# Written instruction lists for four queues of a fused GateLoop and multiplicative-FFN kernel

## The chip, the cores and the metric

The kernel runs on one NeuronCore of a Trainium2 chip. The metric is the device time of one execution in microseconds. A core has five engines that fetch instructions from queues of their own, each strictly in the order in which the queue stands: TensorE (PE, whose weight loads are shown as PEld), VectorE (DVE), ScalarE (ACT), GpSimd (POOL) and SyncE (SP), which here only issues transfers. An instruction that waits for a semaphore holds up everything behind it on its own queue. Transfers that SP and POOL issue are carried out by the same 16 DMA engines.

## The reference, cut to what matters

Two blocks follow each other. The first is a gated linear recurrence with complex gates, for 4 batches, 8 heads, 768 steps and a head width of 48; the second is a feed-forward block whose two products are multiplied element by element.

```
mag = sqrt(a_re**2 + a_im**2)
scale = minimum(mag, 0.999) / (mag + 1e-06)
a_re_n, a_im_n = a_re * scale, a_im * scale
for t in range(S):                      # S_re, S_im: 48 x 48 per head
    new_re = ar * S_re - ai * S_im
    new_im = ar * S_im + ai * S_re
    S_re, S_im = new_re + k[t] v[t]^T, new_im
    y[t] = q[t] @ S_re
x = y, heads beside each other          # 3072 x 384
h = (x @ w1) * (x @ w2) @ w3            # d_ff = 1024
out = h @ w_out
```

The products of w3 and w_out are joined once, since nothing stands between them, so a token costs three matrix products.

## The kernel before, in words

A **unit** is one half of one batch's sequence: 384 steps, all 8 heads. There are 8 units, numbered from 0. Three kinds of work belong to a unit.

**Gates** (`gates` for units 0 and 1, `gates_apart`, lines 598 to 768, from unit 2 on). From the gates `re` and `im` of a unit the kernel makes, on ACT and DVE in turn, the running magnitude and the running angle: logarithm and exponentials on ACT, scans on DVE, then cosine and sine on ACT. The steps that are named later are, in their order: `im_` (L645, im times the reciprocal of re) and `sq_` (L647), `n_` (L653), `min_` and the magnitude scans (L664, L667), `z4_` and `r2_` (L675, L677), the angle scans (L686), `k_` (L702, k times the reciprocal magnitude), `z5_` (L708, the angle cut to one turn, from which ACT at L636 makes abs, cos and sin), `q_` (L716), and four products: `kc_` (L750, k times cosine, tile gR), `qc_` (L753, q times cosine, tile gA), `ks_` (L758, k times sine, in k) and `qs_` (L764, q times sine, in q). Each is done in two parts, one of 384 and one of 768 elements per partition.

**Attention** of a unit on PE: transposes of gR and k (`tp`, L991, copied to KT by ACT at L993), the state products (`kv`, L1069, added to T by DVE at L1075), the scores (`sc`, L1004, whose masked copy to A is DVE's COPY_PREDICATED at L1007), and the outputs (`y`, L1043, copied by ACT and DVE to x0 and x1 at L1047 and L1050; POOL makes x2 at L1051).

**Feed-forward** of a unit on PE: the products `m` (L1089), with evictions by ACT (L1123, L1130) and DVE (`ab`, L1105), and the products `o` (L1184), copied by ACT (L1188) and written out. PE does the feed-forward of unit u-1 while the other engines prepare the gates of unit u.

Once per unit, gR, k, gA and q are moved into a layout by head: twelve transfers on SP (L740) into KL and QL, which the scores read. The unit's v is loaded into `vr` by POOL's queue (L569) and spread by seven more SP transfers into `V` (L591), which `y` reads. The next unit's `re` and `im` come over SP (L527); the next unit's k and q over POOL's queue, released when the last `y` of the unit before has been read.

From unit 3 on the feed-forward uses weights that are split in two parts. The split (`split_ops`, L1152 on ACT, L1155 and L1157 on DVE) runs once, while unit 2 is prepared.

What sets the order: PE's queue is written out by hand as one sequence of pieces. For the other queues the program steps through that sequence and keeps a clock for each engine; `fill`, `fits` and the cost tables (TIMES, WIDE, SCAN, PASS) decide behind which PE piece the next gate step is put, and a table (PLAN) does so for the first 36 pieces. Inside `tc.manual_schedule` the order in which the program text is run is the order of the queue. Before that block, in the stage that joins w3 and w_out and makes unit 0's gates, a scheduler orders the four queues.

Of the kernel before, what the change touches and what calls it, by code (L numbers as in the profile page):

```python
# [21 lines left out]
ORDER = mybir.DependencyInfo(mybir.DependencyClass.NoSync, mybir.DependencyReason.DATA)  # L22
# [352 lines left out]
        f()  # L375


@with_exitstack
def kernel(
    ctx: ExitStack,  # L380
# [32 lines left out]

    nc = tc.nc
    B, H, D, S = qt.shape
    P = 128
    C = 128
# [32 lines left out]
    weights_pool = ctx.enter_context(tc.tile_pool(name="weights", bufs=1))  # L452
    w3o = weights_pool.tile([P, KF, DM], FP, name="w3o")
    ident = weights_pool.tile([P, P], FP, name="ident")
    make_identity(nc, ident)
    good = weights_pool.tile([1, 1], I32, name="good")

    fast = ExitStack()
# [81 lines left out]
    def take(u, x):  # L540
        t = slot(u, x, x)
        g_t.setdefault(u, {})[x] = t[:, :, 0:TT] if x == "q" else t
# [54 lines left out]
    chained, paced = [], []  # L597

    def chain(ins):

        if chained and not paced:
            tc.add_manual_dep(ins.ins, chained[-1].ins.name, ORDER, reason="tables")
        chained[:] = [ins]

    def gate_head(u):
# [762 lines left out]
    def rounding():  # L1368

        stack = ExitStack()  # L1370
        for n, k in (("raw", 2), ("low", 2), ("w3s", 2), ("early", 1)):
            cv[n] = stack.enter_context(tc.tile_pool(name=n, bufs=k))
        return stack
# [25 lines left out]
    def w12_early():  # L1399
        if w1.dtype != FP:  # L1400
            w12_load(0, slice(0, 2), ("q", "k"))
# [23 lines left out]
    def row_load(f, parts=1):  # L1425

        step = FF // parts
        w3_t[f] = fetch([columns(w3t, 0, step)[:, f:f + 1], words(wo)[:, f:f + 1]] +
                        [columns(w3t, n * step, (n + 1) * step)[:, f:f + 1] for n in range(1, parts)],
                        {0: "KL", 1: "QL"}.get(f % 4))  # L1430
# [306 lines left out]
    with tc.manual_schedule(engines={mybir.EngineType.PE}):  # L1737

        phase = rounding()
        row_load(0, 4)  # L1740
        load_gates(0)
        row_load(1, 2)
        row_load(2)
        row_load(3)
        take(0, "q")
        take(0, "k")
        steps = gates(0, True)
        for f in range(KF):
            row_work(f)
            if f == 0:  # L1750
                load_of(0, "k")
                load_of(0, "q")
            if f + 4 < KF:
                row_load(f + 4)
            if f == VLOAD:
                load_v(0)
                w12_early()
            if f == KF - 1:
                continue
            for j in range(KF):  # L1760
                fuse(f, j)
            step(steps, (3, 2, 2, 2, 1, 1, 0)[f])
        for _ in steps:
            pass
        for j in range(KF // 2):
            fuse(KF - 1, j)
        fills = [("f7", lambda j=j: [fuse(KF - 1, j + x) for x in range(2)]) for j in range(KF // 2, KF, 2)]
        gate["ops"] = gates(1, False)
        chain(nc.scalar.preload_act_table_set("natural_log_exp_and_others"))
        with tc.manual_schedule(engines={mybir.EngineType.Activation, mybir.EngineType.DVE, mybir.EngineType.Pool, mybir.EngineType.SP}):  # L1770

            paced.append(True)
            clock.update(PE=0.0, ACT=0.0, DVE=0.0, POOL=0.0, SP=3.0, DMA=8.0)
            landings[:] = [0.0] * RING
            ready.clear()
            ready.update({"moves": 9.0, ("raw", 0): 0.0, ("re", 1): 2.0})
            w12_load(0, slice(len(got) and got[0][0][0].stop, KD))
            turn_v(0)
            w12_load(1)
            rest = ffn(0)  # L1780
            urgent.append([None, w12_ops()])

            def head(i):
                if i % 4 == 0:
                    force(i // 4)
                rest[i][1]()
                if i == HEAD - 1:
                    phase.close()
                    late.append(fast.enter_context(tc.tile_pool(name="late", bufs=1)))
                    late.append(fast.enter_context(tc.tile_pool(name="looks", bufs=1)))  # L1790
                    looks.append(check_weights(late[1]))
                    ops = split_ops()
                    splitting.append([next(ops), ops])
            seq = mixed([x for p in pieces(0) for x in p], fills, FILLS[0]) + [("begin", 0)] + [(rest[i][0], lambda i=i: head(i)) for i in range(HEAD)]
            for u in range(1, NU):
                seq += unit(u, rest[HEAD:] if u == 1 else ffn(u - 1), AHEAD[u])
            seq += ffn(NU - 1)
            advance()
            run(seq[:-4] + [("judge", 0)] + seq[-4:-2] + [("judge", 1)] + seq[-2:])
    fast.close()  # L1800

    value = nc.values_load(good[0:1, 0:1], min_val=0, max_val=1)
    with tc.If(value == 0):
        general(tc, qt, kt, v, art, ait, w1, w2, w3t, wo, w3o, ident, out)

# [35 lines left out]
```

## Time and profile before

| | before |
|---|---|
| median of 3 runs | 534.02 us |
| range of the runs | 533.82 to 536.47 us |
| profiled execution: first to last instruction | 534.5 us |
| PE busy | 498.3 us, 93% |
| DVE busy | 374.7 us, 70% |
| ACT busy | 325.6 us, 61% |
| POOL busy | 254.0 us, 48% |
| mean granted TensorE clock | 0.993 |

The profiled execution's own time is known as its span; the median of the unprofiled runs is 0.5 us below it. A row of a timeline reads: start, length, engine, line, operation, output<-inputs, sizes, count, and in brackets the idle time of that engine just before the row with what ended it. Busy times of PE are modelled at a matmul's end, so a short wait can be hidden in them.

### The profile page before, as it was taken

The page shows a single profiled execution, that of the slowest core. Times are in us where ns is not written, and L with a number is a line of the kernel's source. Part 1 is how long each engine was busy: PE and PEld are TensorE (multiplying, and loading weights), DVE is VectorE, ACT ScalarE, POOL GpSimd, SP SyncE. Part 2 cuts the span into 40 slices and gives each one's busy share as a digit, 9 for nine tenths or more (in the row PEclk, how much of TensorE's full clock was granted, in tenths as well). Part 3 has the DMA queues.
Part 4 walks back from the last instruction along what each step waited for, and adds up shares of the span by engine and source line. Part 5 has one row for each costly group of instructions (what it writes and reads, how often), then busy time and mean ns, then how long its engine had stood idle before and what let it go on. Part 6 is the DMA issues. An engine that isn't in the chain of part 4 may idle for free.

```text
span 534.5 us, 13643 instructions
## 1 busy us (share of the span) xinstructions
PE 498.3 (93%) x5594; PEld 378.1 (71%) x5594; DVE 374.7 (70%) x607; ACT 325.6 (61%) x569; POOL 254.0 (48%) x317
## 2 busy tenths in 40 slices
PE   5689889999998999988999999999999998999995
PEld 2355565556655679957888688967896787878972
DVE  7999699855779988756773876577657837336750
ACT  6979866665675458982587557855786554213420
POOL 1000000028968886752664765487457458415510
PEclk9899999999999999998999999999999999999999
DMA  8999859692379219791599239932993176716611
GB/s 258 369 400 286 189 161 307 126 232 72 79 174 229 73 56 234 157 219 40 126 236 216 77 82 245 225 90 70 229 232 87 40 209 169 205 43 189 200 50 37
DMA packets 66424, 89.75 MB, mean 168 GB/s; under 512 B 29872, under 2 KB 53872, under 8 KB 65584
## 3 DMA queue, kind: packets, MB, share of 16 engines
q1 hardware_dynamic: 57904, 59.15, 44.0%
q0 software_dynamic: 8448, 29.63, 20.3%
q8 instruction: 46, 0.75, 0.6%
q14 instruction: 26, 0.21, 0.1%
HBM read 61.01 MB, written 4.72 MB: 123 GB/s over the span
## 4 chain that ended last, share of the span: by engine, by line
PE 51%; DVE 17%; DMA 13%; issue 6%; ACT 5%; POOL 5%; SPq 1%; POOLq 0%; DVEq 0%; ACTq 0%
PE m L1089 24%; PE o L1184 16%; PE y L1043 4%; PE sc L1004 4%; DMA k<-in_k_dram 3%; DMA KL<-k 3%; PE kv L1069 2%; DVE gR L750 2%; PE tp L991 2%; DMA QL<-q 2%; DMA q<-in_q_dram 2%; DMA look<-in_a_re_dram 1%; DVE gA L753 1%; DMA raw<-in_w_dram 1%; POOL look L1327 1%
## 5 line engine op out<-in xcount | busy, mean ns | idle before, releaser
L1184 PE MATMUL o<-w3o,ab 128*128 128x384 f32 x384 | 131.7, 492 | 0.0
L1089 PE MATMUL m<-x,low 128*128 128x384 f32 x576 | 119.2, 339 | 0.0
L1089 PEld LDWEIGHTS m<-x,low 128*128 128x128 f32 x576 | 102.6, 188 | 0.2 <-ACT m L1123 0.2
L1184 PEld LDWEIGHTS o<-w3o,ab 128*128 128x128 f32 x384 | 70.4, 190 | 45.6 <-issue 2.4
L1105 DVE TENSOR_TENSOR ab<-m,ab 128x384 f32<-128x384 f32 x64 | 35.1, 553 | 57.2 <-PE m L1089 39.4
L1089 PE MATMUL m<-x,wh 128*128 128x384 f32 x288 | 69.6, 350 | 3.4 <-ACT ab L1130 2.4
L1123 ACT ACTIVATE m<-m 128x384 f32<-128x384 f32 x96 | 45.5, 476 | 36.0 <-PE m L1089 35.6
L1089 PE MATMUL m<-xT,ws 128*128 128x384 f32 x192 | 63.1, 487 | 1.2 <-ACT xT L1054 1.2
L1328 POOL TENSOR_SCALAR look<-look 128x192 f32<-128x192 f32 (+1 forms) x55 | 54.4, 988 | 5.0
L1089 PEld LDWEIGHTS m<-x,wh 128*128 128x128 f32 x288 | 50.8, 188 | 7.4 <-ACT ab L1130 3.6
L1325 POOL TENSOR_TENSOR look<-look 128x256 f32<-128x256 f32 (+1 forms) x43 | 31.9, 743 | 50.1 <-DMA look<-in_w_dram 32.3
L1089 PEld LDWEIGHTS m<-xT,ws 128*128 128x128 f32 x192 | 36.0, 190 | 25.6 <-ACT xT L1054 1.7
L1273 POOL MEMSET seen<- 128x256 bf16 x1 | 0.3, 317 | 107.7 <-DVE ab L1105 107.7
L1007 DVE COPY_PREDICATED A<-mask,sc 128x512 f32<-128x512 uint8 x48 | 32.8, 734 | 26.5 <-PE sc L1004 26.5
L1289 POOL TENSOR_TENSOR seen<-seen,look 128x192 bf16<-128x192 bf16 (+1 forms) x55 | 44.3, 805 | 4.5
L1051 POOL TENSOR_TENSOR x<-x,x 128x384 fp32r<-128x384 f32 x18 | 23.1, 1284 | 41.7 <-DVE x L1050 41.5
L1188 ACT COPY ot<-o 128x384 f32<-128x384 f32 x24 | 11.4, 476 | 48.4 <-PE o L1184 48.2
L1043 PE MATMUL y<-A,V 128*32 128x128 f32 x768 | 40.2, 276 | 0.6 <-issue 0.6
L1004 PEld LDWEIGHTS sc<-QL,KL 96*32 96x32 f32 x1536 | 29.2, 112 | 13.6 <-issue 8.7
L1004 PE MATMUL sc<-QL,KL 96*32 96x32 f32 (+3 forms) x1536 | 32.8, 238 | 4.4 <-DMA QL<-q 3.0
L1043 PEld LDWEIGHTS y<-A,V 128*32 128x32 f32 x768 | 35.0, 112 | 1.5 <-issue 1.5
L1043 PE MATMUL y<-QL,T 96*32 96x128 f32 x640 | 35.6, 275 | 0.0
(163 smaller groups left out, 909.2 us busy)
## 6 DMA issues: line engine op xcount, KB each, us to landing
looked<-in_w_dram POOLq DMA_DIRECT2D x14, 512.0 KB, 4.5
look<-in_w_dram POOLq DMA_DIRECT2D x27, 256.0 KB, 5.0
raw<-in_w_dram SPq DMA_DIRECT2D x6, 1024.0 KB, 10.3
KL<-gR SPq DMA_DIRECT2D x24, 192.5 KB, 3.6
KL<-k SPq DMA_DIRECT2D x24, 192.5 KB, 7.1
QL<-gA SPq DMA_DIRECT2D x24, 192.0 KB, 8.2
QL<-q SPq DMA_DIRECT2D x24, 192.0 KB, 7.9
raw<-in_w_dram SPq DMA_DIRECT2D x6, 768.0 KB, 6.1
```

The costliest lines, as they stand in the source:

```text
L1004: nc.tensor.matmul(out=sc[SB * g:SB * g + SB, j, s0:C], lhsT=KL[:, x * n + j, w][:, s0:s0 + SB], rhs=QL[:, x * n + j, w][:, s0:C], start=T ...
L1007: last["sc", u, c, x] = nc.vector.copy_predicated(out=A[:, x * n:(x + 1) * n], data=sc, mask=mask)
L1043: nc.tensor.matmul(out=o, lhsT=a, rhs=b, start=s0, stop=s1)
L1051: nc.gpsimd.tensor_tensor(out=x[2], in0=x[1], in1=x[0], op=OP.subtract)
L1089: nc.tensor.matmul(out=out, lhsT=a, rhs=b, start=start and i == 0, stop=i == len(terms) - 1, skip_group_check=not start)
L1105: last["ab", u, j] = nc.vector.tensor_tensor(out=ab_t[u][:, j], in0=m, in1=ab_t[u][:, j], op=OP.mult)
L1123: nc.scalar.activation(out=got[m], in_=got[m], func=AF.Copy, scale=1.0 + 1.0 / BITS)
L1184: nc.tensor.matmul(out=m, lhsT=ab_t[u][:, f, t * P:(t + 1) * P], rhs=w3o[:, f], start=(f == 0), stop=(f == KF - 1))
L1188: nc.scalar.copy(out=o, in_=m)
L1289: nc.gpsimd.tensor_tensor(out=seen[:, 0:n], in0=seen[:, 0:n], in1=x, op=OP.add)
L1325: tt(out=x, in0=x, in1=x, op=OP.mult)
L1328: ts(out=x, in0=x, scalar1=low, scalar2=None, op0=OP.is_ge)
```

## The change

Each call on ScalarE, VectorE, GpSimd and SyncE now goes through a small recording layer (`Logged`, `Log`), which keeps the instructions of each queue in the order in which the program text made them. The block that put these four queues in that order is gone, and so is the rule that chained ACT's table-dependent instructions. In its place stand written lists, one for each queue: a number n > 0 takes the n-th instruction of those that are left, a number -n takes the next n as they stand. `in_order` ties each instruction to the one before it in the list, with a dependency that costs no semaphore. All recorded instructions have the line of the recording layer, L385. The computation, the tiles, the transfers and their sizes are the same.

```diff
+class Log:
+    def __init__(self, engine):
+        self.engine, self.log = engine, []
+    def __getattr__(self, name):
+        def call(*args, **kw):
+            self.log.append(getattr(self.engine, name)(*args, **kw))
+            return self.log[-1]
+        return call
...
+ORDERS = dict(
+    scalar="""
+9 -15 3 3 3 -2 1 1 1 1 -4 2 -5 8 8 -2 3 -2 1 -9 4 -1 3 -4 6 6 6 -2 4 -1 3 3 3 3 -4 4 -99 5 -2 1 2 -5 1 -4 1 -4 1 -1
...
+""", gpsimd="""
+
+""", sync="""
+-99 8 8 7 9 9 8 -2 4 6 6 7 7 5 5 1 1 -9 4 4 1 1 -4 2 2 1 2 2 1 2 2 1 -5 7 7 7 8 8 8 9 9 -1 9 9 7 7 -1 4 1 1 -7 8 8 7
...
+def in_order(tc, log, order):
+    left, before, taken = list(log), None, []
+    for n in map(int, order.split()):
+        taken += [left.pop(n)] if n > 0 else [left.pop(0) for _ in range(-n)]
+    for ins in taken + left:
+        if before:
+            tc.add_manual_dep(ins.ins, before.ins.name, ORDER, reason="order")
+        before = ins
...
-    nc = tc.nc
+    plain, nc = tc.nc, Logged(tc.nc)
...
-        if chained and not paced:
-            tc.add_manual_dep(ins.ins, chained[-1].ins.name, ORDER, reason="tables")
         chained[:] = [ins]
...
-        with tc.manual_schedule(engines={mybir.EngineType.Activation, mybir.EngineType.DVE, mybir.EngineType.Pool, mybir.EngineType.SP}):
+        if True:
...
+    for name, order in ORDERS.items():
+        in_order(tc, getattr(nc, name).log, order)
```

Lined up instruction by instruction, PE's queue and POOL's queue stand as they did. ACT, DVE and SP stand as they did up to the gates of unit 2; from there on they differ.

The first place is **SP's queue in unit 3**, where gR, k, gA and q are moved. Before:

```order
L591 DMA V<-vr 96x6x48
L740 DMA KL<-gR 16x8x385 x3
L527 DMA im<-in_a_im_dram 128x3x384
L740 DMA KL<-k 16x8x385 x3
L740 DMA QL<-gA 16x8x384 x3
L740 DMA QL<-q 16x8x384 x3
```

and now:

```order
L385 DMA V<-vr 96x6x48 x2
L385 DMA KL<-gR 16x8x385
L385 DMA V<-vr 64x6x48 x2
L385 DMA V<-vr 32x6x48 x2
L385 DMA KL<-gR 16x8x385 x2
L385 DMA KL<-k 16x8x385 x3
L385 DMA QL<-gA 16x8x384 x3
L385 DMA QL<-q 16x8x384 x3
L385 DMA im<-in_a_im_dram 128x3x384
```

The load of unit 4's im has gone from the fourth place behind the V pieces to the last, and four of the seven V pieces stand behind the first gR move.

The second place is **DVE's queue where unit 4's four products are made** (`ab` is the feed-forward eviction of unit 3, which waits for PE). Before:

```order
L691 COPY st_ang<-gZ 128x9
L702 TENSOR_TENSOR k<-k,gR 128x384
L702 TENSOR_TENSOR k<-k,gR 128x2x384
L708 SCALAR_TENSOR_TENSOR gZ<-re,gZ 128x384
L1105 TENSOR_TENSOR ab<-m,ab 128x384
L708 SCALAR_TENSOR_TENSOR gZ<-re,gZ 128x768
L1105 TENSOR_TENSOR ab<-m,ab 128x384
L716 TENSOR_TENSOR q<-q,gA 128x384
L716 TENSOR_TENSOR q<-q,gA 128x2x384
L1105 TENSOR_TENSOR ab<-m,ab 128x384
L750 TENSOR_TENSOR gR<-k,re 128x384
L753 TENSOR_TENSOR gA<-q,re 128x384
```

and now:

```order
L385 COPY st_ang<-gZ 128x9
L385 SCALAR_TENSOR_TENSOR gZ<-re,gZ 128x384
L385 SCALAR_TENSOR_TENSOR gZ<-re,gZ 128x768
L385 TENSOR_TENSOR k<-k,gR 128x2x384
L385 TENSOR_TENSOR ab<-m,ab 128x384
L385 TENSOR_TENSOR k<-k,gR 128x384
L385 TENSOR_TENSOR gR<-k,re 128x384
L385 TENSOR_TENSOR gR<-k,re 128x2x384
L385 TENSOR_TENSOR k<-k,gZ 128x384
L385 TENSOR_TENSOR ab<-m,ab 128x384
L385 TENSOR_TENSOR q<-q,gA 128x2x384
L385 TENSOR_TENSOR k<-k,gZ 128x2x384
```

`z5_` (gZ<-re,gZ) has moved ahead of the products with k, and the products that make gR and k ahead of those with q; one `ab` instead of three stands ahead of gR.

The third place is **DVE's queue at the start of unit 4's gates**, which falls into unit 3's attention (T is the state, A the masked scores). Before:

```order
L1075 TENSOR_TENSOR T_122<-kv,T_124 96x8x48
L645 TENSOR_TENSOR im<-im,re 128x384
L647 ISA gZ,st_tan<-im 128x384
L647 ISA st_tan 128x1
L645 TENSOR_TENSOR im<-im,re 128x768
L647 ISA gZ,st_tan<-im 128x768
L647 ISA st_tan 128x1
L653 SCALAR_TENSOR_TENSOR gA<-gZ,gA 128x384
L1075 TENSOR_TENSOR T_123<-kv,T_122 96x8x48
L653 SCALAR_TENSOR_TENSOR gA<-gZ,gA 128x2x384
L1007 COPY_PREDICATED A_91<-mask,sc_86 128x512
```

and now:

```order
L385 TENSOR_TENSOR T_122<-kv,T_124 96x8x48
L385 TENSOR_TENSOR T_123<-kv,T_122 96x8x48
L385 TENSOR_TENSOR im<-im,re 128x768
L385 TENSOR_TENSOR im<-im,re 128x384
L385 ISA gZ,st_tan<-im 128x768
L385 ISA st_tan 128x1
L385 COPY_PREDICATED A_91<-mask,sc_86 128x512
```

The products with im now stand behind the second state sum, directly ahead of the masked copy of the first scores; the second square and `n_` stand behind that copy.

More of the change, by code (lines that the diff above doesn't have):

```diff
@@ L375, in general, with __init__, __getattr__ @@
         f()
+class Log:
[6 more added lines that the diff above has]
+        return call
+class Logged:
+    def __init__(self, nc):
+        self.nc = nc
+        self.scalar, self.vector, self.gpsimd, self.sync = (Log(e) for e in (nc.scalar, nc.vector, nc.gpsimd, nc.sync))
+    def __getattr__(self, name):
+        return getattr(self.nc, name)
+ORDERS = dict(
+    scalar="""
[19 rows of a table added]
+""")
+def in_order(tc, log, order):
[6 more added lines that the diff above has]
+        before = ins
 @with_exitstack
@@ L454 @@
     ident = weights_pool.tile([P, P], FP, name="ident")
-    make_identity(nc, ident)
+    make_identity(plain, ident)
     good = weights_pool.tile([1, 1], I32, name="good")
@@ L1799 @@
             run(seq[:-4] + [("judge", 0)] + seq[-4:-2] + [("judge", 1)] + seq[-2:])
+    for name, order in ORDERS.items():
+        in_order(tc, getattr(nc, name).log, order)
     fast.close()
-    value = nc.values_load(good[0:1, 0:1], min_val=0, max_val=1)
+    value = plain.values_load(good[0:1, 0:1], min_val=0, max_val=1)
     with tc.If(value == 0):
```

15 rows, old and new, of the table scalar are left out of this document.

## The prediction, on record before the run

> **What bounds the kernel now.** I read the page first, for the engine that is full.
>
> ```profile
> span 534.5 us, 13643 instructions
> PE 498.3 (93%) x5594; PEld 378.1 (71%) x5594; DVE 374.7 (70%) x607; ACT 325.6 (61%) x569; POOL 254.0 (48%) x317
> ```
>
> PE is full and no other engine comes near. PE's own instructions stand in the same order after the change, so a new order on the other queues can only return what PE loses by waiting, or add to it. Next I read whom PE waits for from 105 us to the end; before that the order is the old one.
>
> ```profile
> PE sc L1004 <- DMA QL<-q: 3.0, 1, 3.0
> PE kv L1069 <- ACT KT L993: 2.9, 2, 2.2
> PE m L1089 <- ACT ab L1130: 2.4, 3, 1.0
> PE tp L991 <- DVE gR L750: 1.6, 3, 0.7
> PE tp L991 <- DVE k L758: 1.0, 2, 0.7
> PE m L1089 <- DVE ab L1105: 0.8, 2, 0.4
> PE sc L1004 <- DVE A L1007: 0.6, 2, 0.3
> ```
>
> Columns: total us, times, longest. That is 12.3 us: one wait of 3.0 for a transfer, one of 2.2 for a copy on ACT, and many of at most 1.0. Last I read busy times by stage; the last three columns are granted clock, DMA share and GB/s.
>
> ```profile
> 140.00:200.00 60.00, 57.82 (x653) 37.28 (x652) 49.80 (x67) 33.64 (x57) 47.92 (x54) 1.00 0.56 134
> 200.00:240.00 40.00, 38.42 (x281) 32.88 (x279) 28.59 (x41) 33.87 (x61) 26.74 (x33) 1.00 0.90 203
> 240.00:245.00 5.00, 3.11 (x124) 2.98 (x128) 1.92 (x3) 0.46 (x1) 2.14 (x3) 0.84 0.19 68
> 245.00:250.00 5.00, 5.00 (x87) 4.01 (x78) 4.45 (x8) 1.43 (x3) 0.42 (x1) 0.81 0.02 3
> ```
>
> Of these stretches the clock is below 1.00 only in the two around and behind the longest wait: 5 x (1 - 0.84) + 5 x (1 - 0.81) = 1.75 us of PE's work is lost there. About 14 us, 2.6%, is all that can be had.
>
> **Term 1, unit 3's transfers: -2.98 and -1.75.** PE and SP there, then DVE:
>
> ```profile
> 241.58 1.32 PE L1004 MATMUL sc<-QL,KL 96*32 96x128 f32 x64 [2.98 <-DMA QL<-q]
> ...
> 210.14 6.40 SPq L591 DMA_DIRECT2D V<-vr  x7
> 220.67 2.74 SPq L740 DMA_DIRECT2D KL<-gR  x3
> 223.54 0.60 SPq L527 DMA_DIRECT2D im<-in_a_im_dram  x1
> ...
> im<-in_a_im_dram SPq DMA_DIRECT2D x7, 576.0 KB, 7.2
> ```
> ```profile
> 222.08 1.44 DVE L753 TENSOR_TENSOR gA<-q,re 128x768 f32<-128x768 f32 x1
> 223.91 1.85 DVE L758 TENSOR_TENSOR k<-k,gZ 128x384 f32<-128x384 f32 x2
> ```
>
> The scores waited from 238.60 to 241.58 for the last QL piece, while the transfer engines were 0.90 busy at 203 GB/s. The load of im, 576 KB or 0.59 MB, stood ahead of nine of the twelve moves. At 203 GB/s it takes 2.9 us of that stretch; put last, it lets QL land 2.9 us sooner, at about 238.7. The k products now also stand ahead of the last q product (1.44), so the KL moves of k start over 1 us earlier. The price is that four of the seven V pieces, 4/7 of 6.40 or 3.7 us of issue, now stand between the gR moves; but the second of these waited for DVE anyway, so I set that at no more than the gain from the k products. The wait goes, and with it, as I read the rows, the 1.75 us of clock that follow it. In unit 2 and in units 4 to 7 no wait for QL stands in the list, so moving im there is worth nothing by itself.
>
> [...]
>
> **Term 2, units 4 to 7, the waits for gR, k and the two ab: -5.8.** That is 1.6 + 1.0 + 2.4 + 0.8 from the list. Unit 4 shows how they arise:
>
> ```profile
> 264.42 1.46 DVE L702 TENSOR_TENSOR k<-k,gR 128x384 f32<-128x384 f32 x2 [1.04 <-DMA k<-in_k_dram]
> 265.80 0.54 DVE L708 SCALAR_TENSOR_TENSOR gZ<-re,gZ 128x384 f32<-128x384 int32 x1
> 266.74 0.94 DVE L708 SCALAR_TENSOR_TENSOR gZ<-re,gZ 128x768 f32<-128x768 int32 x1
> 269.41 0.56 DVE L1105 TENSOR_TENSOR ab<-m,ab 128x384 f32<-128x384 f32 x1 [1.74 <-ACT re L636]
> 269.89 1.42 DVE L716 TENSOR_TENSOR q<-q,gA 128x384 f32<-128x384 f32 x2
> 272.60 0.56 DVE L1105 TENSOR_TENSOR ab<-m,ab 128x384 f32<-128x384 f32 x1 [1.29 <-ACT gZ L636]
> 273.07 0.86 DVE L750 TENSOR_TENSOR gR<-k,re 128x384 f32<-128x384 f32 x1
> 274.33 1.55 DVE L750 TENSOR_TENSOR gR<-k,re 128x768 f32<-128x768 f32 x1
> ...
> 269.65 0.93 ACT L636 ACTIVATE re<-re,consts 128x768 f32<-128x768 f32 x1
> ...
> 275.93 0.44 PE L991 MATMUL tp<-ident,gR 128*128 128x128 f32 x2 [0.67 <-DVE gR L750]
> ```
>
> The angle scans ended at 263.2; `z5_` waited behind the k product, and that for k's landing at 264.4. The cosine was ready at 269.65 + 0.93 = 270.6, but both gR products ended only at 275.9, behind two `ab` that wait for PE and behind q. Now `z5_` starts at 263.4 and takes 0.54 + 0.94, to 264.9 instead of 267.7, so the cosine comes 2.8 us sooner, at 267.8. Ahead of gR stand only k (1.46) and one `ab` (0.56), done by 267; gR ends at about 267.8 + 0.86 + 1.55 = 270.2. PE stood waiting for it from 275.93 - 0.67 = 275.3: 5 us to spare. The same `z5_` held abs on ACT, and `ab` (L1130) behind it, in the three waits of 2.4. I count all four kinds as gone.
>
> What pays for this is the start of the gates, which moves back:
>
> ```profile
> 232.54 0.56 DVE L645 TENSOR_TENSOR im<-im,re 128x384 f32<-128x384 f32 x1 [0.72 <-DMA im<-in_a_im_dram]
> 235.97 0.55 DVE L1075 TENSOR_TENSOR T<-kv,T 96x384 f32<-96x384 f32 x1
> 236.58 0.96 DVE L653 SCALAR_TENSOR_TENSOR gA<-gZ,gA 128x768 f32<-128x768 f32 x1
> 242.43 1.35 DVE L1007 COPY_PREDICATED A<-mask,sc 128x512 f32<-128x512 uint8 x2 [4.89 <-PE sc L1004]
> 246.13 0.34 DVE L664 TENSOR_SCALAR gA<-gA 128x384 f32<-128x384 f32 x1
> ```
>
> Before, the im work began at 232.5 and `n_` ended at 237.5. Now it begins behind the second T, at 236.5, and three instructions (0.95, 0.56, 0.96) end at 239.0; the first masked copies wait for the scores to about 239.9 and take 1.35; the second square, the next copies and `n_` follow, to about 245. The next step, `min_`, ran at 246.13 before, since the copies stood ahead of it. So the delay of 7 us at `n_` is nearly gone one step later, if im has landed by 236.5.
>
> **Term 3, unit 2's wait for KT: 0, between -2.2 and 0.**
>
> ```profile
> 154.52 0.55 DVE L1105 TENSOR_TENSOR ab<-m,ab 128x384 f32<-128x384 f32 x1
> 166.69 0.94 DVE L1155 SCALAR_TENSOR_TENSOR low<-ws,wh 128x768 fp32r<-128x768 f32 x1
> 167.67 0.84 ACT L1152 ACTIVATE wh<-ws 128x768 fp32r<-128x768 f32 x1 [0.71 <-DVE low L1155]
> 168.42 0.54 ACT L993 COPY KT<-tp 128x384 f32<-128x384 f32 x1
> 169.01 0.88 PE L1069 MATMUL kv<-vr,KT 128*32 128x48 f32 x48 [2.17 <-ACT KT L993]
> ```
>
> The second KT copy stands behind a weight split on ACT that waits for DVE's third `low`; in the new lists it still stands behind that same split. DVE's `ab` of 154.52 now stands ahead of half of gR and of all later products, and PE gives it no sooner, so DVE reaches that `low` at about the same time. I take 0.
>
> **Term 4, new waits: +1.9, between 0 and +6.** The trace cannot show a wait that the new order makes. Below nothing it cannot be, by definition of the term. The nearest row is PE's wait for a masked copy, 0.6 in two times, 0.3 each, which is the kind of wait that im work ahead of a copy makes; one for each of the six units 2 to 7 gives 1.9. The upper end is six of 1.0, the largest wait for DVE or ACT in units 4 to 7.
>
> **Sum.** 534.5 - 2.98 - 1.75 - 5.8 + 0 + 1.9 = 525.9 for the profiled execution; the runs' median lies 0.5 below its span, so **525.5 us**, 1.6% faster.
>
> **The rivals.** [...] *The lists fit other times than the chip's*: DVE and ACT meet waits at other places, and half of terms 1 and 2 comes back: 525.5 + 5.3 = 530.8. For it: unit 2's `ab` above, where the new order also stands and waits. Against it: 5 us to spare in unit 4. *It does not do what it says, since transfers bound the units*: at 0.90 busy QL lands no sooner, whatever the order; term 1 stays (4.73), and the 2.6 saved at tp are lost again at sc: 525.5 + 4.7 + 2.6 = 532.8. For it the 0.90, against it the 0.56 in 140 to 200.
>
> *Slower*: one mechanism, im as the last transfer. If it lands with the last piece as QL does now, at 241.3 instead of 232.5, then DVE stands at `im_` from 236.5 on, with the masked copies behind it: they start at 241.3 + 0.95 + 0.56 + 0.96 = 243.8 instead of 239.9, and PE's `y` waits 3.9 us. In units 3 and 6 the lists have im and the first square ahead of the first copies: +7.8. The gate chain then starts later by more than the 5 us to spare, and term 2's 5.8 come back: 525.5 + 7.8 + 5.8 = 539. It decides from im landing later than 236.5 in unit 3. Against it: the moves ahead of im start earlier too, and in units 4 and 5 a copy stands ahead of im.
>
> **How the numbers follow.** Forecast 525.5: 0.50; clock: 0.08; half back: 0.15; transfers: 0.13; slower: 0.14. Only a difference over 0.5% (2.7 us) can be told from no change, so faster 0.50 + 0.08 + 0.15 = 0.73, same 0.13, slower 0.14. Low end: all 12.3 and 1.75 gone, 520, hardly reached, so 520.5; the high end takes in the third rival and stops short of the last, 535. The forecast's own range is 521 to 529.
>
> **What would show it.** Right: no wait of over 1 us of PE at sc in unit 3 and a clock of 1.00 there; gR's rows some 5 us ahead of tp in unit 4; the 2.2 for KT still there. Wrong: DVE waiting for im ahead of a masked copy, PE waiting in `y`, or a list of PE's waits from 105 us on that sums to over 8 us.

## The result, and the profile after

The changed kernel took 531.02 us, the median of 20 runs (523.93 to 541.33), beside 537.18 us (533.43 to 540.35) for the kernel before, measured with it. The ratio is 0.985, 95% interval 0.982 to 0.989: faster by 1.5%. This ratio leaves out runs that are more than 1.5% above the fastest of their kernel, 8 of the changed kernel's 20 and none of the 20 before; the two medians over all runs give 0.989, faster by 1.1%. The forecast, 525.5 against 534.02, was a ratio of 0.984.

The profiled execution has these first lines; the order is that of the profile before.

```profile
span 527.4 us, 13622 instructions
PE 495.9 (94%) x5594; PEld 377.1 (72%) x5594; DVE 372.4 (71%) x607; ACT 324.7 (62%) x569; POOL 257.5 (49%) x317
```

PE's list of waits from 105 us on, with total, times and longest. In the changed kernel nearly all recorded instructions of the other engines have line L385, and PE's lines have moved by 56.

```profile
PE m L1145 <- DVE ab L385: 2.1, 2, 1.9
PE m L1145 <- ACT ab L385: 1.9, 3, 0.8
PE m L1145 <- ACT m L385: 1.0, 1, 1.0
PE kv L1125 <- ACT KT L385: 0.7, 1, 0.7
PE sc L1060 <- DVE A L385: 0.6, 2, 0.3
PE m L1145 <- ACT xT L385: 0.6, 1, 0.6
PE tp L1047 <- DVE T L385: 0.2, 1, 0.2
```

That is 7.1 us; the same list of the kernel before sums to 13.5, since the prediction's 12.3 leaves out its three smallest rows (0.6, 0.4 and 0.2). The waits for QL (3.0), gR (1.6) and k (1.0) are gone, and so is unit 2's for KT (2.2); the 0.7 that is left is unit 1's, which both kernels have. In their place stand waits that the kernel before did not have: 1.9 for an `ab` of VectorE, 1.0 for an `m` copy and 1.9 for `ab` copies of ScalarE.

The kernel before, the changed kernel and the experiments below have one order ahead of unit 2's gates, and still their profiled executions come to the end of that part up to 11 us apart (142.8 to 153.8 us). So from here on the stretch behind it is compared. It begins with the products `m` behind unit 1's xT and ends with PE's last product. First the kernel before, then the changed one, PE's timeline:

```profile
138.82 5.11 PE L1089 MATMUL m<-xT,ws 128*128 128x384 f32 x15 [0.60 <-ACT xT L1054]
...
525.75 2.74 PE L1184 MATMUL o<-w3o,ab 128*128 128x384 f32 x8
```
```profile
141.43 4.78 PE L1145 MATMUL m<-xT,ws 128*128 128x384 f32 x14 [0.57 <-ACT xT L385]
...
518.68 2.74 PE L1240 MATMUL o<-w3o,ab 128*128 128x384 f32 x8
```

From the first to the last row it took 389.7 us before (525.75 + 2.74 - 138.82) and 380.0 us now: 9.7 us less, where the spans differ by 7.1. The other 2.6 were lost ahead of it, where the order of every queue is the same in both. Since PE's instructions stand in one order in both kernels, each can be set against itself, and the difference of the starts shows where time was won and lost:

| PE instruction | before | now | now - before | step |
|---|---|---|---|---|
| unit 1's m, behind xT | 138.82 | 141.43 | +2.6 | |
| kv behind KT, unit 2 | 169.01 | 169.38 | +0.4 | -2.2 |
| m behind an ab, at the start of unit 3 | 208.03 | 210.42 | +2.4 | +2.0 |
| first scores of unit 3 | 241.58 | 241.00 | -0.6 | -3.0 |
| y of unit 3 | 246.87 | 244.74 | -2.1 | -1.5 |
| tp of k, unit 4 | 292.00 | 290.12 | -1.9 | +0.2 |
| m, unit 5 | 323.84 | 321.01 | -2.8 | -0.9 |
| m, unit 6 | 380.13 | 376.00 | -4.1 | -1.3 |
| tp of k, unit 7 | 449.41 | 442.60 | -6.8 | -2.7 |
| PE's end | 528.49 | 521.42 | -7.1 | -0.3 |

Two things stand out. The gain at KT was lost again 40 us later. And unit 4 gained nothing, although both gR and k came in time there. The busy times by stage show the step of -1.5 (last three columns: granted clock, DMA share, GB/s):

```profile
200.00:240.00 40.00, 37.90 (x280) 32.57 (x279) 24.61 (x33) 24.92 (x46) 26.89 (x32) 1.00 0.89 199
240.00:245.00 5.00, 4.69 (x176) 3.81 (x178) 4.70 (x10) 1.31 (x2) 4.40 (x6) 1.00 0.17 62
245.00:250.00 5.00, 5.00 (x119) 3.46 (x111) 4.68 (x7) 4.53 (x9) 2.91 (x3) 1.00 0.10 38
```

Behind unit 3's scores the granted clock is 1.00, where it was 0.84 and 0.81. The transfer engines are as busy ahead of them as before, 0.89 at 199 GB/s.

### The profile page after: what moved, and what is told of

It reads as the page before. It is cut to its first block, busy times and chain, and to the rows that moved or that the text cites. A ratio compares the mean times of both kernels' runs of the same rounds, so it can differ in the third digit from the quotient of the medians.

```text
span 527.4 us, 13622 instructions
## 1 busy us (share of the span) xinstructions
PE 495.9 (94%) x5594; PEld 377.1 (72%) x5594; DVE 372.4 (71%) x607; ACT 324.7 (62%) x569; POOL 257.5 (49%) x317
## 4 chain that ended last, share of the span: by engine, by line
PE 46%; DVE 17%; DMA 13%; POOL 12%; issue 7%; ACT 3%; SPq 2%; POOLq 0%; DVEq 0%; ACTq 0%
PE m L1145 20%; PE o L1240 14%; POOL look L385 9%; DMA re<-in_a_re_dram 6%; DVE gZ L385 4%; DMA look<-in_a_re_dram 3%; PE y L1099 3%; DVE gA L385 3%; PE sc L1060 3%; DVE gR L385 2%; PE kv L1125 2%; POOL seen L385 2%; SPq L385 2%; PE f L1507 2%; PE tp L1047 1%
## 5 line engine op out<-in xcount | busy, mean ns | idle before, releaser
L385 POOL TENSOR_SCALAR look<-look 128x192 f32<-128x192 f32 (+1 forms) x70 | 74.7, 1067 | 16.3 <-DMA look<-in_a_re_dram 10.8
L385 DVE TENSOR_TENSOR ab<-m,ab 128x384 f32<-128x384 f32 x64 | 35.4, 554 | 63.4 <-PE m L1145 53.0
L385 POOL TENSOR_TENSOR look<-look 128x256 f32<-128x256 f32 (+1 forms) x58 | 43.8, 755 | 50.4 <-DMA look<-in_w_dram 32.3
L385 ACT ACTIVATE m<-m 128x384 f32<-128x384 f32 x96 | 45.7, 478 | 33.0 <-PE m L1145 32.4
L385 POOL MEMSET seen<- 128x256 bf16 x1 | 0.3, 316 | 110.1 <-DVE ab L385 110.1
L385 ACT COPY ot<-o 128x384 f32<-128x384 f32 x24 | 11.4, 476 | 61.4 <-PE o L1240 61.3
L385 POOL TENSOR_TENSOR seen<-seen,look 128x192 bf16<-128x192 bf16 (+1 forms) x55 | 42.7, 776 | 4.5
L385 DVE COPY_PREDICATED A<-mask,sc 128x512 f32<-128x512 uint8 x48 | 32.7, 734 | 11.6 <-PE sc L1060 11.5
L385 POOL TENSOR_TENSOR x<-x,x 128x384 fp32r<-128x384 f32 x18 | 24.2, 1350 | 34.3 <-DVE x L385 34.3
L385 ACT COPY ab<-m 128x384 f32<-128x384 f32 x64 | 30.5, 477 | 16.3 <-PE m L1145 16.1
L385 ACT ACTIVATE low<-raw 128x384 uint16<-128x384 uint32 (+6 forms) x40 | 33.9, 888 | 6.1 <-DMA raw<-in_w_dram 3.1
```

What stands on the lines that cost most here:

```text
L385: self.log.append(getattr(self.engine, name)(*args, **kw))
```

## The experiments

Two small additions to the order of a list are used below. `MOVES` takes the instruction at one position of a queue's list and puts it in at another; `FORMER` puts a stretch of positions back into the former order. "1290th" is PE's 1290th instruction, 4 us into the first row above: to PE's end it was 385.7 us before and 376.0 us in the changed kernel. The last column sums PE's waits on that stretch. The last two columns come from one profile of each run; in the two profiles of the changed kernel (its own and e9) they differ by 1.0 and 0.8 us.

| run | edit | ratio to the kernel before, 95% interval | 1290th to end, us | waits, us |
|---|---|---|---|---|
| the kernel before | | | 385.7 | 12.1 |
| the changed kernel | | 0.985 (0.982 to 0.989) | 376.0 | 5.6 |
| e1 | SyncE's list alone | 1.044 (1.034 to 1.053) | 411.3 | 29.6 |
| e2 | ScalarE's and VectorE's lists alone | 0.993 (0.989 to 0.998) | 376.9 | 7.0 |
| e3 | im back in unit 3 | 0.982 (0.972 to 0.992) | 383.0 | 11.1 |
| e4 | four new waits mended | 0.989 (0.981 to 0.996) | 377.1 | 5.6 |
| e5 | unit 2's products in former order | 0.988 (0.982 to 0.994) | 379.5 | 7.2 |
| e6 | angle step behind k, units 4 to 7 | 1.001 (0.996 to 1.005) | 383.5 | 9.8 |
| e7 | products in former order, units 4 to 7 | 1.009 (1.005 to 1.013) | 391.7 | 15.4 |
| e8 | waits for k and re moved back | 0.988 (0.983 to 0.993) | 381.5 | 7.6 |
| e9 | the changed kernel again | medians 535.82 and 537.13: 0.998, no interval | 375.0 | 4.8 |
| e10 | k load of unit 4 earlier | 0.988 (0.983 to 0.993) | 378.5 | 7.4 |
| e11 | the same, and ScalarE | 0.983 (0.977 to 0.989) | 378.0 | 6.5 |
| e12 | k load of unit 3, and ScalarE | 0.978 (0.970 to 0.986) | 376.7 | 5.2 |

### Which list ended the wait for QL (e1, e2, e3)

An instruction that a list does not take follows in the order of the program text, which is the former order. So a list cut off ahead of unit 2's gates gives a queue its former order back.

```diff
 # e1: ScalarE and VectorE in the former order
-... 3 3 3 3 -4 4 -99 5 -2 1 2 -5 1 -4 1 ...
+... 3 3 3 3 -4 4 -99
-... 2 -1 1 2 -4 3 -100 1 -1 5 3 2 6 4 1 ...
+... 2 -1 1 2 -4 3
 # e2: SyncE in the former order
--99 8 8 7 9 9 8 -2 4 6 6 7 7 5 5 1 1 ...
+-99
 # e3: the changed kernel, unit 3's im behind its three KL<-gR
+MOVES = {'sync': [(142, 133)]}
```

> Only SyncE's new list is kept; ScalarE and VectorE follow the former order in units 2 to 7. Theory A, the prediction's first term (im in front of nine moves is what made unit 3's scores wait): with im last the last QL piece lands 2.9 us sooner, PE's wait of 2.98 us at sc is gone or under 0.5, the granted clock behind it is 1.00, every other wait of the kernel before stays (KT 2.2, gR 1.6, the two ab): 534.5 - 4.7, ratio to the kernel before about 0.991. Theory B (the changed kernel's QL moves were issued earlier because VectorE makes the products earlier; 227.8 there against 233.7 before for the last one): with VectorE's former order the moves are issued as late as before, the wait stays over 2 us with the low clock, ratio about 1.00.

> The reverse: ScalarE's and VectorE's new lists, SyncE in the former order with im ahead of nine moves. Theory A: unit 3's wait for QL stays at 2 to 3 us with the low clock of 1.75 us behind it; KT (2.2) and the waits for gR, k and the two ab of units 4 to 7 (5.8) are gone; the new waits of the changed kernel (1.9 at unit 3's start, 1.0 and 0.8 in unit 4, 0.9 in unit 5) are there: 527.4 + 4.5 = about 532, ratio 0.993. Theory B: the QL wait is gone here too, span about 527, ratio 0.985.

> The changed kernel with one transfer moved: unit 3's im stands again behind its three KL<-gR moves, ahead of the KL<-k and QL moves. Theory A: PE waits about 3 us at sc in unit 3 again and the clock falls behind it: span 527.4 + 4.5 = 532, ratio 0.993. Theory B: the last QL piece landed at 236.2 and the scores began at 241.0, so 2.9 us more for im in front (239.1) still leave 1.9 us to spare: no wait at sc, span 527, ratio 0.985 as for the changed kernel.

**e1** came out as neither theory had it: 4.4% slower. PE's timeline at unit 3's scores, then SyncE's and VectorE's:

```profile
248.61 1.32 PE L1048 MATMUL sc<-QL,KL 96*32 96x128 f32 x64 [1.02 <-DMA QL<-q]
256.40 2.36 PE L1048 MATMUL sc<-QL,KL 96*32 96x128 f32 x64 [6.46 <-DVE A L385]
```
```profile
238.73 1.98 SPq L385 DMA_DIRECT2D QL<-q  x3
240.75 0.61 SPq L385 DMA_DIRECT2D im<-in_a_im_dram  x1
```
```profile
250.72 0.56 DVE L385 TENSOR_TENSOR im<-im,re 128x384 f32<-128x384 f32 x1 [9.89 <-DMA im<-in_a_im_dram]
...
255.63 1.34 DVE L385 COPY_PREDICATED A<-mask,sc 128x512 f32<-128x512 uint8 x2
```

The wait for QL shrank from 2.98 to 1.02, so the place of im is worth some 2 us where the products come as late as before (the last q product ends 11.3 us ahead of PE's turn for the scores, before 11.0). But im itself now lands at 250.6, 3.0 us behind PE's turn. VectorE in its former order takes im ahead of the masked copies, stands still for 9.89 us, and PE waits 6.46 for the copies behind it. Over the whole stretch VectorE waits for im four times, by its list of waits:

```profile
DVE im L385 <- DMA im<-in_a_im_dram: 38.4, 4, 12.0
```

This is the mechanism of the slower rival, at the place that it named. In the first profile of the changed kernel it did not come up: im was issued earlier, since the products were done earlier, and landed at 238.00, 3.0 us ahead of the scores; VectorE took it at 238.82, right behind the second T, without a wait. The margin is thin. In e9, the second profile of the same kernel, im landed 0.9 us ahead of the scores, VectorE waited for it ahead of the masked copies, and PE waited 1.21 us for these, where the first profile has 0.31:

```profile
243.71 1.79 DVE L385 TENSOR_TENSOR im<-im,re 128x768 f32<-128x768 f32 x2 [1.27 <-DMA im<-in_a_im_dram]
```
```profile
247.08 1.38 PE L1060 MATMUL sc<-QL,KL 96*32 96x128 f32 x64 [1.21 <-DVE A L385]
```

**e2** has SyncE's former order, im ahead of nine moves, and still no wait for QL in unit 3. SyncE, the last q product on VectorE, then PE:

```profile
219.65 0.61 SPq L385 DMA_DIRECT2D im<-in_a_im_dram  x1
...
224.83 2.38 SPq L385 DMA_DIRECT2D QL<-q  x3
```
```profile
220.84 0.57 DVE L385 TENSOR_TENSOR q<-q,gZ 128x384 f32<-128x384 f32 x1
```
```profile
238.93 1.32 PE L1059 MATMUL sc<-QL,KL 96*32 96x128 f32 x64
```

The last QL move is issued by 227.2, where the kernel before got to it at 233.1 to 233.7, since VectorE has its products done sooner: the last one ended at 221.4, before at 227.6. It landed at 236.0, 2.9 us ahead of the scores, and the granted clock is 1.00 from 200 to 300 us. **e3** says the same: with im back in front, the last QL piece landed at 252.8 and the scores began at 256.1 without a wait. Its longer stretch is not from there: PE waited 4.7 at unit 3's start for the same `ab` as in the changed kernel, and 2.5 for GpSimd's x, 32 and 40 us ahead of the scores.

So theory B holds for the wait that I had put down to im: VectorE's and ScalarE's order ends it alone (which of the two lists is needed was not run). The place of im does some of it where those stay as they were, and then costs far more than it brings. What SyncE's list adds within the full change is small: in e2 PE waits once more for QL, 1.0 us in unit 5, and the stretch is 0.9 us longer than the changed kernel's first profile, 1.9 longer than its second. The ratios say less than the rows here: e2's 0.993 is the number that theory A gave, for a wait that is not there, and its interval and the changed kernel's meet at 0.989. By the ratios SyncE's list would be worth 0.8%, so its size stays open.

### Unit 2's wait for KT (e5)

```diff
 # the changed kernel, VectorE's 23 instructions from the k products to the second split in former order
+FORMER = {'vector': [(211, 234)]}
```

> The changed kernel with VectorE's former order in unit 2 from the k products to the second weight split (23 instructions). Theory: PE's 2.2 us for KT went because VectorE gets to the splits (low) earlier: its first three ran at 158.2, 162.2, 165.5 with PE 2.6 us late, against 161.9, 164.0, 166.7, that is 6.3, 4.4 and 3.8 us sooner; with the former order the wait of about 2.2 comes back and everything behind it is 2.2 later. Rival: ScalarE's own list does it (its first split of the weights stands 2.6 us sooner, ahead of two gate activations); then the wait at KT stays at 0.7 or less.

The wait is back, at 2.7 us; PE's timeline, and VectorE's for the third split:

```profile
170.26 0.88 PE L1129 MATMUL kv<-vr,KT 128*32 128x48 f32 x48 [2.70 <-ACT KT L385]
```
```profile
167.54 0.96 DVE L385 SCALAR_TENSOR_TENSOR low<-ws,wh 128x768 fp32r<-128x768 f32 x1 [0.19 <-ACT wh L385]
```

In the changed kernel, where the splits stand between the products and PE came to this place 1.8 us later than here, the same split ran 2.0 us earlier:

```profile
165.50 0.95 DVE L385 SCALAR_TENSOR_TENSOR low<-ws,wh 128x768 fp32r<-128x768 f32 x1
```

ScalarE's split ahead of the second KT copy waits for the third. Two things bring VectorE there sooner: the first split stands five products earlier in the new list, and the q products stand later, so that VectorE no longer waits for q's transfer, 1.22 us in the kernel before and 1.29 in e5. The rival, ScalarE's own list, was left in and did not help. A second thing shows in e5: with the KT wait back, the `ab` wait of 1.9 at unit 3's start is gone.

### Term 2's two parts (e6, e7)

```diff
 # e6: k, k, angle step, angle step, ab in units 4 to 7 (was: angle step ahead of k)
+MOVES = {'vector': [(330, 328), (332, 329), (383, 381), (385, 382), (436, 434), (489, 486), (490, 487)]}
 # e7: VectorE's former order from k_ to qs_ in units 4 to 7
+FORMER = {'vector': [(328, 345), (381, 399), (433, 450), (486, 504)]}
```

> The changed kernel with the two k products of units 4 to 7 again ahead of the angle step (z5_) on VectorE; gR and k stay ahead of q. Theory A, the prediction's second term with both its parts: the cosine comes 1.4 to 2.5 us later, gR of unit 4 ends at about 269.5 and still 3.5 us ahead of PE's tp (273.2), so the waits for gR and k stay gone, but ScalarE's ab copies stand late behind abs again: three waits of 0.6 to 1.0, 2.4 in all, span + 2.4. Theory B: the order of the products does it all (k products landed and done earlier in this kernel): no wait for ab of ScalarE beyond those the changed kernel has (0.83 and 0.85), span + 0.

> The changed kernel with VectorE's whole former order from the k products to the last q product in units 4 to 7. Theory: VectorE's order is the cause of term 2: waits for gR (1.6), k (1.0), VectorE's ab (0.8) and some of ScalarE's ab (2.4) come back, 3.4 to 5.8 in all, on top of the waits that the changed kernel has on ScalarE in units 4 and 5. Rival: ScalarE's list, which runs the cosine and the sine copies earlier, is enough, and less than 2 us come back.

In **e6** no wait for gR or k came back, but waits for ScalarE did, as theory A has it, and larger: the stretch is 7.5 us longer where 2.4 were expected. Most of it is one place, unit 7. VectorE, then PE:

```profile
431.26 1.43 DVE L385 TENSOR_TENSOR k<-k,gR 128x768 f32<-128x768 f32 x2 [4.02 <-DMA k<-in_k_dram]
```
```profile
434.14 1.33 PE L1149 MATMUL m<-x,low 128*128 128x384 f32 x3 [2.84 <-ACT m L385]
```

VectorE stood 4.0 us at k with the angle step behind it, ScalarE stood at abs with an `m` copy behind that, and PE waited 2.84; with it the granted clock was low for 6.8 us (0.50 from 434 to 440 us). In **e7** the waits for k and gR are back too:

```profile
PE tp L1051 <- DVE k L385: 1.9, 3, 0.7
...
PE tp L1051 <- DVE gR L385: 0.9, 2, 0.5
```

2.8 us for k and gR were 2.6 in the kernel before. So the order of the products (gR and k ahead of q, with fewer `ab` ahead of them) ends the waits at `tp`, and the angle step ahead of k ends those for ScalarE. Which of the two, q or the `ab`, held gR longer was not run apart. VectorE's former order with ScalarE's new list is worse than the former order of both (the stretch is 391.7 against 385.7): the two lists were made for each other.

### The new waits (e4, e8 to e12)

Three of the new waits in the changed kernel, with what stands ahead of them. At unit 3's start, on VectorE, GpSimd and PE:

```profile
208.94 0.96 DVE L385 TENSOR_TENSOR k<-k,gR 128x768 f32<-128x768 f32 x1 [2.34 <-DMA k<-in_k_dram]
209.82 0.55 DVE L385 TENSOR_TENSOR ab<-m,ab 128x384 f32<-128x384 f32 x1
```
```profile
199.29 4.31 POOL L385 TENSOR_TENSOR x<-x,x 128x384 fp32r<-128x384 f32 x3
203.54 0.81 POOL L385 DMA_DIRECT2D k<-in_k_dram  x1
```
```profile
210.42 0.79 PE L1145 MATMUL m<-x,wh 128*128 128x384 f32 x3 [1.91 <-DVE ab L385]
```

In unit 4, on ScalarE and PE:

```profile
272.88 1.26 ACT L385 ACTIVATE gA<-re,consts 128x1152 f32<-128x1152 f32 x1 [3.60 <-DMA re<-in_a_re_dram]
...
274.14 0.47 ACT L385 ACTIVATE m<-m 128x384 f32<-128x384 f32 x1
```
```profile
274.66 0.79 PE L1145 MATMUL m<-x,low 128*128 128x384 f32 x3 [0.96 <-ACT m L385]
276.29 0.80 PE L1145 MATMUL m<-x,wh 128*128 128x384 f32 x3 [0.83 <-ACT ab L385]
```

Each time an instruction that waits for a transfer stands ahead of a copy that PE needs, and that the kernel before had ahead.

```diff
 # e4
+MOVES = {'vector': [(275, 274)], 'scalar': [(306, 305), (308, 307), (377, 376)]}
 # e8
+MOVES = {'vector': [(275, 274), (281, 278)]}
+FORMER = {'scalar': [(243, 248), (305, 316), (374, 384), (437, 444)]}
```

> The changed kernel with the four largest waits that it has and the kernel before had not taken at their source, as read in its trace: on VectorE one ab at 209.82 is put ahead of the k product that stood waiting for a transfer until 208.94; on ScalarE, in units 4 and 5, two activations of re (which waited for re's transfer until 272.88 in unit 4) no longer stand ahead of one m copy and two ab copies. Theory: these places alone make the waits of 1.91, 0.96, 0.83 and 0.85 us, so about 4.5 us go, span about 523, ratio to the kernel before 0.977. Rival: PE is held at these places by more than the one instruction (ScalarE's m copies behind the scans, the next transfer), and less than half returns: span 525.5 or more, ratio 0.981 or more.

> A second try at the new waits. The first showed that a wait only went to the next instruction behind the same transfer: k of unit 3 landed at 214.5, and the ab behind the angle step and T came 1.1 us late; re's landing stood ahead of the next ab on ScalarE. Now two ab of unit 3 stand ahead of the k products' wait and of the angle step on VectorE, and ScalarE follows its former order from the last m copies to the table load in units 3 to 6, where the re activations stand behind ab and KT. Theory: what the changed kernel still waits for from unit 2 on (5.5 us behind the xT wait of unit 1) is made by instructions that wait for a transfer ahead of copies that PE needs; 4 us or more go, and from that xT wait to PE's end it takes 377 to 378 us against 381 in the changed kernel; ratio to the kernel before about 0.977. Rival: the later re activations start the next gates late, and waits at other places take it back: 380 us or more.

**e4**: the rival. The `ab` that I moved came in time, and PE waited 1.1 for the next one, which stands behind the angle step and T behind the same k. ScalarE met re again in units 3, 4 and 6. The sum stayed at 5.6. **e8** won from unit 4 on (3.2 us less than the changed kernel from unit 3's state products to the end), but PE waited 2.4 for GpSimd's x and another 4.3 for VectorE and ScalarE in unit 3, and the clock fell twice, to 0.50 in 211 to 214 us and again from 224.2 on.

```diff
 # e9: nothing changed
 # e10
+MOVES = {'gpsimd': [(124, 118), (119, 124), (119, 124), (119, 124)]}
 # e11: the same, and
+MOVES = {'vector': [(275, 274)]}
+FORMER = {'scalar': [(305, 316), (374, 384), (437, 444)]}
 # e12: ScalarE as in e11, and
+MOVES = {'gpsimd': [(86, 80)]}
```

> The changed kernel unaltered, beside the next two, so that they are compared with it and not only with the kernel before. From the first matmul of unit 2's m on (the 1290th instruction of PE) to PE's end it took 376.0 us in its first profile; all theories expect 375 to 378 here and a ratio to the kernel before of about 0.985.

> The changed kernel with one change on GpSimd, ahead of unit 3: the load of k and the three subtractions x - x stand ahead of the last scan of a weight piece (look) instead of behind it. In the changed kernel GpSimd issued k's load at 203.54, behind 2.8 us of look and 4.3 us of x; it landed at 208.9, and PE waited 1.91 us. Theory: the wait at unit 3's start hangs on when GpSimd issues that load; issued 7 us sooner it lands at about 203, ahead of the end of the scans (206.6), and the 1.9 us go: 374 us from the 1290th instruction on. Rival: the list's ab also stands behind scans, and PE still waits over 1 us there.

> The same, with one ab of unit 3 ahead of the k products on VectorE, and with ScalarE in its former order from the last m copies to the table load in units 4, 5 and 6 (in the trial before, the part from unit 4 on became 3.2 us shorter by it, and unit 3 longer). Theory: both gains add, 1.9 and 2 to 3 us: 371 to 373 us from the 1290th instruction on against 376 in the changed kernel, ratio to the kernel before about 0.976. Rival: what is gained at one place is waited for at the next transfer: 375 or more, and no difference to the changed kernel that the runs can tell.

> The two runs before moved the load of k of unit 4 instead of unit 3's (unit 3's wait stayed at 2.1 and 1.5, and a new one of 1.24 came in unit 4). Here the load of k of unit 3 alone is put ahead of the last scan of a weight piece and of the three subtractions x - x on GpSimd, some 6 us sooner than in the changed kernel (203.54 there), and ScalarE follows its former order from the last m copies to the table load in units 4, 5 and 6. Theory: k lands at about 203 ahead of the end of the scans, the wait of 1.9 at unit 3's start is gone, and in units 4 to 6 the waits of 0.96, 0.83, 0.85 and 0.2: from the 1290th instruction of PE to its end 371 to 373 us against 376.0 and 375.0 in the two profiles of the changed kernel. Rival: each of these waits comes again at the next transfer or the next engine, 375 us or more, no difference to the changed kernel that the runs can tell.

**e9**, the same kernel, took as long on the stretch (375.0 against 376.0), but the median of its six runs is 0.998 of the kernel before, where 0.985 was expected; its profiled run lost 6.1 us ahead of the stretch against the first profile. It had no wait at all at unit 3's start. There PE came 6.1 us later than in the first profile, and GpSimd's load of k only 1.9 us later (205.47). Set against PE's 1950th instruction, some 25 matmuls ahead of the wait, the load was issued 4.2 us earlier in the kernel before, 4.6 in e9 and 5.3 in e5, and in these three there is no such wait. It was issued 0.4 us earlier or less in the first profile, e2, e6 and e7, and there the wait is 1.8 to 2.3 us; in e3 it was issued 3.3 us later, and the wait is 4.7. GpSimd's queue stands in the same order in all of these and scans pieces of weights at its own pace, 3.3 us and more for a piece (3.39 from 192.38 to 195.77 in the changed kernel). What makes it early or late against PE within one kernel was not settled.

**e10** and **e11** tell nothing on that, since I had moved the load of the wrong unit; they added a wait of 1.24 in unit 4 each. **e12** has the right one, and the load was issued at 197.60. The wait for `ab` is gone, and another has come:

```profile
202.15 4.92 POOL L385 TENSOR_TENSOR x<-x,x 128x384 fp32r<-128x384 f32 x3
```
```profile
207.12 1.33 PE L1152 MATMUL m<-x,low 128*128 128x384 f32 x3 [3.69 <-POOL x L385]
```

The x products that PE needs stand on GpSimd behind a scan that could wait. That the move made this wait is not shown: e3 and e8, where GpSimd's order is the changed kernel's, have it too, 2.5 and 2.4 us. From unit 4 on ScalarE's waits are down to 0.5 us, from 2.9 in the changed kernel, and from unit 3's state products to the end it is 2.2 and 3.7 us shorter than the two profiles of the changed kernel. Its ratio, 0.978, is the lowest of all, but its interval overlaps the changed kernel's; that it is faster is not shown. A version with x and k both ahead of that scan was not run.

## Why the prediction was right, and where not

**The time** was right: a ratio of 0.985 against 0.984, the span 527.4 against 525.9, of which 2.6 us were lost ahead of the changed part. Behind it the sum of the terms was -8.6 and the measured change -9.7. By the medians over all runs the ratio is 0.989, and 531.02 us lies above the forecast's own range of 521 to 529; the kernel before, too, took 537.18 in these runs and not 534.02. That the sum came so near is in part luck: terms 3 and 4 were off by -2.2 and +3.1.

**Term 1, size right, cause wrong.** -4.73 was forecast, -3.0 - 1.5 were measured, and what was to show it (no wait over 1 us at sc in unit 3, a clock of 1.00) is there. The step that failed is "put last, it lets QL land 2.9 us sooner": e3 puts im back and no wait follows, e2 never moves it and none follows. I had seen the k products ahead of the last q product and allowed "over 1 us" for them. In e2, with SyncE's order as before, the last QL move was issued 6.5 us sooner (227.2 against 233.7), while PE reached the scores at the same time (238.9 against 238.6). e1 gives im's own share where the products come late, 2 us of 2.98; with the new products it is nothing at this place (e2, e3). The size could not tell the causes apart: whatever ends the wait gives back its 2.98.

**The clock** went as the rows before said: the wait of 2.98 is gone, and with it the low clock behind it. For a clock that stays low for 1.75 us all the same, to which the forecast gave 0.08, the changed kernel's profile has no row: from 140 us to the last products, at 521, its granted clock is 1.00.

**Term 2, right.** All four kinds of wait are gone where the kernel before had them (ScalarE's `ab` is waited for at other places: term 4). From `y` of unit 3 to PE's end the table has -5.0; without the 3.0 of new waits on that stretch it would be -8.0, where -5.8 was forecast (the rows that are gone there sum to 6.1, and each gave back somewhat more than its row). Both parts of the mechanism show when undone (e6, e7). Unit 4 went as worked out; VectorE, ScalarE, PE of the changed kernel:

```profile
261.70 1.93 DVE L385 SCALAR_TENSOR_TENSOR gZ<-re,gZ 128x384 f32<-128x384 int32 x2
...
265.53 1.52 DVE L385 TENSOR_TENSOR gR<-k,re 128x384 f32<-128x384 f32 x2
```
```profile
265.12 0.94 ACT L385 ACTIVATE re<-re,consts 128x768 f32<-128x768 f32 x1
```
```profile
273.21 0.49 PE L1047 MATMUL tp<-ident,gR 128*128 128x128 f32 x3
```

gR ended at 267.05, 6.2 us ahead of `tp`, where 5 were forecast. The price, the start of the gates, was right in this profile: im ran at 238.82 without a wait and no masked copy came late. im landed at 238.00 and not by the 236.5 that was asked, but PE was 2.5 us later there, and with it VectorE's second T. In e9 a price was paid: 1.27 us of waiting for im, and 0.9 more at the masked copies.

**Term 3, wrong: -2.2, not 0.** The step was "DVE reaches that `low` at about the same time". I had followed the one `ab` that stands earlier, and not the first `low`, which stands five products earlier, nor the wait for q's transfer. VectorE started the third `low` 3.8 us sooner against PE (165.50, PE being 2.6 late, against 166.69). e5 shows it: with the former order the wait is 2.7.

**Term 4, undersized.** 1.9 was forecast, 0 to 6 allowed. The size was taken from PE's waits for masked copies; the waits that came were of another kind, copies behind an instruction that waits for a transfer. At unit 3's start the table has +2.0, and in units 4 to 7 the new rows sum to 3.0: 5.0 in all. The two errors, -2.2 and +3.1, partly cancel, and they may hang together: in e5, where the wait at KT is back, and in e9 the load of k was issued over 4 us ahead of PE, and there is no wait at unit 3's start. In this profile the gain at KT was lost again there. A small misreading changes nothing: the masked copies began 0.85 us behind the first scores (242.43 against 241.58), so without the wait they would begin at 239.5, not 239.9.

**The rivals.** "The lists fit other times" is what term 4 became at four places, but half of terms 1 and 2 did not come back. "Transfers bound the units" (532.8, which the high end of 535 was set to take in) fell: QL landed in time at the same 0.89 busy. The slower rival fell for the change as it is, where its mechanism cost nothing in one profile and 0.9 us in the other, and is real for one of its parts: e1. The median, 531.02, lies at the price of the half-back rival, 530.8, but what it rested on, half of terms 1 and 2, is not what the trace shows.

## What to carry to other kernels

Where an instruction waits for a transfer, look at what PE needs behind it on the same queue, on each engine that the chain passes; moving one copy ahead only handed the wait to the next copy behind the same transfer here (e4: 1.1 us, where it had been 1.91), and with the transfer itself issued sooner PE met another wait (e12: 3.69 us). Put a queue's order back alone before naming the transfer that ended a wait: here two parts of the change each reached the same wait, and one of them without the others made the kernel 4% slower. Lists for several queues are one piece of work: half of them can be worse than none (e1: 1.044; e7: a stretch of 391.7 us against 385.7).

## What was not expected of the hardware

**The clock.** In these traces it fell in or behind single waits of PE from 2.43 us on, though not at each of them, and was then low for 3.4, 6.8 or 10.2 us. Behind the wait that ended at 241.58 in the kernel before (columns as above, granted clock third from the end):

```profile
243.00:244.00 1.00, 0.79 (x29) 0.79 (x33) 0.78 (x2) 0.00 (x0) 0.00 (x0) 0.72 0.00 0
244.00:245.00 1.00, 1.00 (x40) 1.00 (x36) 0.58 (x1) 0.00 (x0) 0.00 (x0) 0.50 0.00 0
245.00:246.00 1.00, 1.00 (x32) 1.00 (x26) 0.66 (x2) 0.00 (x0) 0.00 (x0) 0.50 0.00 0
246.00:247.00 1.00, 1.00 (x31) 1.00 (x26) 0.90 (x3) 0.00 (x0) 0.00 (x0) 0.57 0.08 16
```

Taken as 0.50 wherever it is low, as the two middle rows have it, these four rows hold 2 x (0.28 + 0.50 + 0.50 + 0.43) = 3.4 us of it, and it began 1.9 us after PE had gone on. At e6's wait of 2.84 it was low for 6.8 us, at e1's of 6.46 for 10.2, in both from before PE had gone on (0.76 at 433 to 434, 0.75 at 252 to 253). Waits of 2.43, 2.70, 2.84, 2.98, 3.46, 3.65, 3.69, 4.68, 5.16 and 6.46 us had it in or behind them, waits of 1.91, 2.08, 2.10, 2.17, 2.28 and 2.54 had not. So the length of one wait does not decide in these runs: 2.43 had it and 2.54 not, and in e8 three waits of 0.63, 0.74 and 1.56 us that ended within 4.4 us of each other were followed by a clock of a half for 3.4 us, from 224.2 on. What sets the moment of the fall, and the 3.4 us, was not shown.

**Five waits that cost more than their rows.** Start against start, the waits of 0.67, 1.03 and 2.98 us that vanished gave 0.84, 1.20 and 3.05 us, and the new ones of 0.83 and 1.91 cost 1.02 and 2.07: 0.1 to 0.2 us more each.

**VectorE beside GpSimd.** In e11, where x fell on another moment, VectorE's product of 0.95 us took 4.03 while GpSimd made its three x products:

```profile
254.44 4.03 DVE L385 TENSOR_TENSOR gZ<-gA,gR 128x768 f32<-128x768 f32 x1 [0.18 <-ACT gR L385]
```
```profile
254.75 2.90 POOL L385 TENSOR_TENSOR x<-x,x 128x384 fp32r<-128x384 f32 x3
```

In the changed kernel, where the three came apart from each other, the same product took 0.95 at 255.22, and the x product that started beside it at 255.38 took 1.65, the one before it 1.25. That the two engines held each other up is an estimate from these rows, and no run shows by what. Why VectorE's product was the long one in the one execution and GpSimd's in the other was not settled.
